# A ConvNeXt-V2 block on one core: rstd by GpSimd's pow, sums of bn_stats on GpSimd, and the yn transfers issued ahead of the input transposes

## The chip, the cores and the metric

The kernel runs on one core of one Trainium2 chip. The metric is the device time in microseconds. Before the change it is 1974.33 us, the median of two runs (1964.08 and 1984.58).

The core has five engines that run their own instruction streams: TensorE (PE in the profile, with PEld for its weight loads), VectorE (DVE), ScalarE (ACT), GpSimd (POOL) and SyncE (SP). Here SP does nothing but issue DMAs and wait on semaphores, in the order of its stream.

## The reference

The input `x` is one image of 512 x 512 pixels with 96 channels, in bf16. What is computed:

```python
out = jnp.zeros_like(x)
for i in range(K):                       # K = 3: a depthwise 3x3 convolution, padded
    for j in range(K):
        out = out + xp[:, i:i+H, j:j+W, :] * dw[i, j][None, None, None, :]
h = _layernorm(out, axis=-1)             # (x - mean) / sqrt(var + 1e-5) over the 96 channels
h = jnp.einsum('bhwc,ce->bhwe', h, w1)   # 96 -> 384
h = _gelu(h)                             # tanh form
gx = jnp.sqrt((h * h).sum(axis=(1, 2), keepdims=True) + 1e-6)   # over all pixels
nx = gx / (gx.mean(axis=-1, keepdims=True) + 1e-6)
h = grn_gamma * (h * nx) + grn_beta + h
h = jnp.einsum('bhwe,ec->bhwc', h, w2)   # 384 -> 96
return x + h
```

The sum in `gx` goes over the whole image, so nothing behind it can start before every pixel has passed the gelu. That splits the kernel into two phases.

## The kernel before

**Blocks and slots.** A block is four image rows (`GR = 4`); there are 128 blocks. Phase 1 is one loop over slots (line 454). Slot s does the convolution of block s and, for earlier blocks, later steps of the pipeline. A table (`at`, lines 422 to 449) gives each step its slot. Every engine's instructions are kept in the order in which the program writes them (the class `InOrder`, lines 25 to 40; the profile puts all of these at line 35). So a step that waits on an engine or on SP holds everything that stands behind it there.

**The steps of phase 1.** In the order of a block's life:

- `load_x` (line 234): SP issues one DMA transpose that brings eight image rows, channels on partitions, into `xT`. One in every second slot, four `xT` buffers; it is issued four slots ahead of the even block with the same rows, and first read by the block before that one.
- `conv_chunks` (line 255): nine taps of 12 matmuls on 32x32 tiles of TensorE add up in one PSUM tile `Y`. `evac` then has ScalarE copy `Y` to `y_bf`, and GpSimd square it into `ysq`. There is one `Y`, so the next convolution waits for its eviction.
- `stage_stats` (line 288): small matmuls sum `y_bf` and `ysq` over channels, into the PSUM tile `S`, for a batch of blocks. Batches have 2, 2, 4 and then 8 blocks (15 of these).
- `stage_chain` (line 302): once per batch VectorE turns the sums into mean and variance, and into rstd by a shift of the float's bits and three Newton steps; then it transposes rstd in 32x32 blocks into `rt`.
- `stage_rows` (line 340): SP writes `rt` to DRAM (four DMAs), one slot after the chain. `stage_bcast` (line 350): SP reads it back onto 32 partitions per image row (four DMAs), two slots later.
- `stage_norm` (line 358): GpSimd multiplies `y_bf` by rstd into `yn`. One slot later `stage_write` (line 366) has SP write `yn` to DRAM, and another slot later `stage_read` (line 369) has SP read it in another layout into one of four `ynT` buffers. The mean's subtraction is folded into the weights `w1p`.
- `mlp_units` (line 376), three slots after the norm: per block six units of two matmuls (96 -> 128 of the 384 features, two image rows), each followed by a gelu on ScalarE into `gt`. After every second unit VectorE takes `bn_stats` of the four rows of `gt`, and, for three blocks in eight (`RECOMP_PATTERN`, line 89: blocks 0, 3 and 6), SP writes `gt` to DRAM. For the others phase 2 computes it again.
- `combine` (line 403): once in eight blocks VectorE turns these statistics into sums of squares.

With batches of eight, block b's MLP is in slot b + 17. Counted modulo 8, the g writes are in slots 1, 4 and 7, the chain in slot 1, the rows in slot 2, the broadcast in slot 4, the combine in slot 0; slot 2 has no channel sums and slot 3 those of two blocks.

**The order within a slot** (lines 457 to 502) is: `load_x` (even slots), writes, reads, broadcasts, norms; then MLP units and convolution taps by turns with the channel sums after the second; then the eviction and `ysq`; then chain, combine and rows. SP therefore sees, in a slot: transpose, yn write, yn read, broadcasts, g writes, rows.

**Phase 2** scales `w2` by the normalisation (lines 512 to 544), loads or recomputes the gelu's output, multiplies by the scaled weights and adds `x`. The change reaches only its first two instructions.

Of the kernel before, what the change touches and what calls it, by code (L numbers as in the profile page):

```python
# [16 lines left out]
NEWTON_ITERS = 3  # L17
LAG_ST = 2
LAG_NORM = 5
LAG_MLP = 3  # L20
# [36 lines left out]
def kernel(  # L57
# [21 lines left out]
    NCH = E // 128  # L79
    NG = W // 128  # L80
    assert H % XR == 0
    NBLK = H // GR
# [80 lines left out]
    NACC = (NBLK + 7) // 8  # L163
    acc = consts.tile([128, NCH, NACC], f32, name="acc")
    nc.vector.memset(acc[:], 0.0)

    grp = {}
    ld_engs = [nc.sync, nc.gpsimd]
# [39 lines left out]
    with ExitStack() as p1:  # L208
# [25 lines left out]
        def load_x(k):  # L234
            lo = k * XR
            xT = xtpool.tile([128, XR, W], bf16, name="xT")
            npix = XR * W
            is_last = lo + XR == H
            npix_t = npix - 16 if is_last else npix
            dst = xT[:].rearrange("p r w -> p (r w)")  # L240
            src = bass.AP(x_t, x_off + lo * W * C, [[C, npix_t], [1, 128]])
            sp.dma_start_transpose(dst[:, 0:npix_t], src)
            if is_last:
                with nc.allow_non_contiguous_dma("last 16 pixels"):
                    sp.dma_start(out=xT[0:C, XR - 1, W - 16:W],
                                      in_=x[0, H - 1, W - 16:W, :].rearrange("w c -> c w"))
            xT_tiles[k] = xT

        ybf, ysq, yns, ynts, rbcs, Ss, rts = {}, {}, {}, {}, {}, {}, {}
        batch_of = {}  # L250
        for k, (b0, n) in enumerate(BATCHES):
            for b in range(b0, b0 + n):
# [47 lines left out]
                                         start=(i == 0), stop=(i == NI - 1))  # L300

        def stage_chain(k):
            b0, n = BATCHES[k]
            N = n * GR * NG
            NT = (N + 31) // 32 * 32
            S = Ss[k]
            mean = small.tile([128, 128], f32, name="mean")
            dve.tensor_scalar(out=mean[:, :N], in0=S[:, 0, :N], scalar1=1.0 / C, scalar2=None, op0=ALU.mult)
            nmsq = small.tile([128, 128], f32, name="nmsq")
            dve.scalar_tensor_tensor(out=nmsq[:, :N], in0=mean[:, :N], scalar=-1.0, in1=mean[:, :N],  # L310
                                           op0=ALU.mult, op1=ALU.mult)
            var = small.tile([128, 128], f32, name="var")
            dve.scalar_tensor_tensor(out=var[:, :N], in0=S[:, 1, :N], scalar=1.0 / C, in1=nmsq[:, :N],
                                           op0=ALU.mult, op1=ALU.add)
            dve.tensor_scalar(out=var[:, :N], in0=var[:, :N], scalar1=0.0, scalar2=LN_EPS,
                                    op0=ALU.max, op1=ALU.add)
            ri = small.tile([128, 128], i32, name="ri")
            dve.tensor_scalar(out=ri[:, :N], in0=var[:, :N].bitcast(i32), scalar1=1, scalar2=None,
                                    op0=ALU.arith_shift_right)
            dve.tensor_scalar(out=ri[:, :N], in0=ri[:, :N], scalar1=-1, scalar2=0x5F3759DF,  # L320
                                    op0=ALU.mult, op1=ALU.add)
            rcur = ri[:, :N].bitcast(f32)
            rn = None
            for it in range(NEWTON_ITERS):
                t_ = small.tile([128, 128], f32, name="nt")
                dve.scalar_tensor_tensor(out=t_[:, :N], in0=rcur, scalar=-0.5, in1=rcur,
                                               op0=ALU.mult, op1=ALU.mult)
                dve.tensor_tensor(out=t_[:, :N], in0=t_[:, :N], in1=var[:, :N], op=ALU.mult)
                rn = small.tile([128, 128], bf16 if it == NEWTON_ITERS - 1 else f32,
                                name="rstd" if it == NEWTON_ITERS - 1 else "rn")  # L330
                dve.scalar_tensor_tensor(out=rn[:, :N], in0=t_[:, :N], scalar=1.5, in1=rcur,
                                               op0=ALU.add, op1=ALU.mult)
                rcur = rn[:, :N]

            rt = rtpool.tile([128, 128], bf16, name="rt")
            dve.transpose(out=rt[:, :NT], in_=rn[:, :NT])
            rts[k] = rt
            Ss.pop(k)

        def stage_rows(k):  # L340
            b0, n = BATCHES[k]
# [61 lines left out]
        def combine(k):  # L403

            bst = bsts.pop(k)
            nr = min(8, NBLK - 8 * k) * GR
            for j in range(NCH):
                v = bst[:, j, :nr, :].rearrange("p a (h s) -> p a h s", h=2)
                sq = small.tile([128, 32, 2], f32, name="sq")
                dve.scalar_tensor_tensor(out=sq[:, :nr, :], in0=v[:, :, :, 1], scalar=256.0, in1=v[:, :, :, 1],  # L410
                                               op0=ALU.mult, op1=ALU.mult)
                sq2 = small.tile([128, 32, 2], f32, name="sq2")
                dve.scalar_tensor_tensor(out=sq2[:, :nr, :], in0=sq[:, :nr, :], scalar=1.0, in1=v[:, :, :, 2],
                                               op0=ALU.mult, op1=ALU.add, accum_out=acc[:, j, k:k + 1])

        def fill(n):
            U = psU.tile([128, 2, W], f32, name="U")
# [6 lines left out]
        def put(s, what):  # L424
            at.setdefault(s, []).append(what)
# [3 lines left out]
        for k, (b0, n) in enumerate(BATCHES):  # L429
            for b in range(b0, b0 + n):  # L430
                s = b + LAG_ST
                if b == b0:
                    s = max(s, last_stat_slot + 2)
                put(max(s, b + LAG_ST), ("stats", b))
                last_s = max(s, b + LAG_ST)
            last_stat_slot = last_s
            put(last_s, ("chain", k))
            put(last_s + 1, ("rows", k))
            put(last_s + 3, ("bcast", k))
            for b in range(b0, b0 + n):  # L440
                s = max(last_norm + 1, last_s + LAG_NORM)
                last_norm = s
                put(s, ("norm", b))
                put(s + 1, ("write", b))
                put(s + 2, ("read", b))
                put(s + LAG_MLP, ("mlp", b))
                last_slot = s + LAG_MLP
                if b % 8 == 7 or b == NBLK - 1:
                    put(s + LAG_MLP, ("combine", b // 8))

        load_x(0)
        load_x(1)
        fill(FILL_FIRST)
        for s in range(last_slot + 1):
            todo = at.get(s, [])
            get = lambda kind: [v for kk, v in todo if kk == kind]
            if s % 2 == 0 and s // 2 + 2 < H // XR:
                load_x(s // 2 + 2)
            for b in get("write"):
                stage_write(b)  # L460
            for b in get("read"):
                stage_read(b)
            for k in get("bcast"):
                stage_bcast(k)
            for b in get("norm"):
                stage_norm(b)
            units = []
            for b in get("mlp"):
                units += mlp_units(b)
            taps, evac = conv_chunks(s) if s < NBLK else ([], None)  # L470
            for b in get("stats"):
                pass
            stats = [lambda b=b: stage_stats(b) for b in get("stats")]

            order = []
            u, t = list(units), list(taps)
            if not u:
                order += t
                if t:
                    order.append(lambda: fill(FILL_EARLY))  # L480
                order += stats
            else:
                k = 0
                while u or t:
                    if u:
                        order.append(u.pop(0))
                    n = 2 - k % 2
                    order += t[:n]
                    t = t[n:]
                    if k == 1:  # L490
                        order += stats
                    k += 1
            for f in order:
                f()
            if evac:
                evac()
            for k in get("chain"):
                stage_chain(k)
            for k in get("combine"):
                combine(k)  # L500
            for k in get("rows"):
                stage_rows(k)

        for q in range(NPRE0):
# [7 lines left out]
    with ExitStack() as pg:  # L512
        gsm = pg.enter_context(tc.tile_pool(name="gsm", bufs=1))
        psG = pg.enter_context(tc.tile_pool(name="psG", bufs=1, space=bass.MemoryType.PSUM))
        ssq = gsm.tile([128, NCH], f32, name="ssq")
        nc.vector.tensor_reduce(out=ssq[:], in_=acc[:], axis=AX.X, op=ALU.add)
        gx = gsm.tile([128, NCH], f32, name="gx")
        nc.scalar.activation(out=gx[:], in_=ssq[:], func=ACTF.Sqrt, bias=eps_t[:], scale=1.0)
        rs_ = gsm.tile([128, 1], f32, name="rs_")
# [101 lines left out]
```

## Time and profile before

One execution was taken by the profiler, with a time of 1976.21 us by the same measure as the runs.

| | us |
|---|---|
| median of the runs | 1974.33 |
| profiled execution | 1976.21 |
| its span, first to last instruction | 1974.2 |
| phase 1, about | 0 to 1400 |
| VectorE busy / in phase 1 | 1672.3 / 1202.1 |
| ScalarE busy / in phase 1 | 1401.3 / 942.2 |
| TensorE (PE) busy / in phase 1 | 1536.8 / 1017.1 |
| GpSimd busy / in phase 1 | 858.3 / 752.5 |
| granted TensorE clock, mean | 0.862 of full speed |

How to read the lines: in a list of groups a row names the engine, the operation, its output and inputs (out<-in, with their shapes), how often it ran, its busy time, its mean duration in ns, and the idle time of the engine before it with what ended that. In a timeline the first two numbers are start and duration in us from the span's start; SPq is a DMA issue on SP, and its duration is that of issuing, not of the transfer. In a table of stretches each row gives, for one stretch, its length and the busy time of each engine with the number of instructions, in the order PE, PEld, DVE, ACT, POOL, then the granted clock, the share of the DMA engines, and GB/s. In a list of waits a row gives us in total and how many times. A busy PE isn't a PE at full speed: a matmul lasts longer at the lower clock.

### The profile page before, as it was taken

The numbers are of one execution on the slowest core, as the hardware profiler recorded it, in microseconds if no ns is written. First come the engines' busy times: TensorE is split into PE (matmuls) and PEld (weight loads), VectorE is DVE, ScalarE is ACT, GpSimd is POOL, SyncE is SP. The second block draws the span as 40 slices with busy tenths as digits, with TensorE's granted clock in tenths as the row PEclk, the third lists the DMA queues.
The fourth block names the chain that finished last, engine by engine and source line by source line (L and its number), as shares of the span: only waits on it lengthen the run. The fifth ranks groups of instructions, "written<-read, shape, count | busy, mean of one in ns | idle before, by whom it ended". The sixth has DMA issues, their size and how long they took to land. (4 is left out here: it accounts for less than half of the span.)

```text
span 1974.2 us, 58644 instructions
## 1 busy us (share of the span) xinstructions
PE 1536.8 (78%) x25396; PEld 687.7 (35%) x25642; DVE 1672.3 (85%) x2646; ACT 1401.3 (71%) x1381; POOL 858.3 (43%) x467
## 2 busy tenths in 40 slices
PE   7577767777777878777777777755599999999998
PEld 4223222222222222222222221211366666666666
DVE  4645998889899898989999999899888888888887
ACT  2455686676777666677686786877578888788887
POOL 5545565645555545565555655551211111112110
PEclk9778797887788777778797897988799999999999
DMA  7878777677675866857778586475699999999995
GB/s 145 167 182 179 204 204 188 177 225 202 179 207 170 221 177 196 221 172 199 195 225 210 172 242 184 155 237 169 236 384 367 366 374 362 376 366 369 371 367 228
DMA packets 466867, 472.17 MB, mean 239 GB/s; under 512 B 292432, under 2 KB 388784, under 8 KB 466608
## 3 DMA queue, kind: packets, MB, share of 16 engines
q1 hardware_dynamic: 414000, 348.86, 60.5%
q0 software_dynamic: 20608, 88.09, 12.0%
q10 hardware_dynamic: 32000, 31.46, 5.1%
q8 instruction: 200, 3.28, 0.7%
q14 instruction: 59, 0.48, 0.1%
HBM read 224.55 MB, written 176.69 MB: 203 GB/s over the span
## 5 line engine op out<-in xcount | busy, mean ns | idle before, releaser
L35 DVE BATCH_NORM_STATS2 bst<-gt 128x6 f32<-128x512 bf16 x1536 | 926.1, 678 | 151.6 <-ACT gt L35 147.7
L35 ACT ACTIVATE gt<-U 128x1024 bf16<-128x1024 f32 x768 | 773.4, 1027 | 372.1 <-PE U L35 166.2
L35 PE MATMUL U<-ynT,w1p 128*128 128x512 bf16 x1307 | 505.8, 462 | 185.4 <-DMA ynT<-yn_dram 145.5
L35 PE MATMUL Y<-xT,Wd 32*32 32x512 bf16 x13806 | 466.4, 450 | 172.7 <-ACT y_bf L35 116.5
L35 POOL TENSOR_TENSOR ysq<-y_bf 128x1536 bf16<-128x1536 bf16 x128 | 351.7, 2748 | 534.5 <-ACT y_bf L35 505.1
L200 ACT ACTIVATE gl<-U 128x1024 bf16<-128x1024 f32 x480 | 457.5, 1028 | 106.0 <-PE U L198 97.5
L35 POOL TENSOR_TENSOR yn<-y_bf,rbc 128x1536 bf16<-128x1536 bf16 x128 | 396.3, 3099 | 29.7 <-DMA yn_dram<-yn 16.8
L570 PE MATMUL O<-W2s,gl 128*128 128x96 bf16 x6096 | 350.4, 206 | 19.8 <-ACT gl L200 5.1
L570 PEld LDWEIGHTS <-gl 128*128 128x128 bf16 x6096 | 304.1, 97 | 140.4 <-ACT gl L200 54.1
L572 DVE TENSOR_TENSOR o_sb<-O,xb 128x384 bf16<-128x384 f32 x512 | 257.1, 552 | 95.8 <-PE O L570 95.6
L35 PEld LDWEIGHTS <-Wd 32*32 32x32 bf16 x13806 | 130.7, 90 | 513.4 <-issue 507.2
L198 PE MATMUL U<-ynl,w1p 96*128 96x512 bf16 x960 | 283.4, 379 | 29.9 <-ACT gl L200 27.8
L184 POOL DMA_DIRECT2D xr<-in_x_dram x127 | 68.6, 540 | 487.5 <-DVE xb L561 371.4
L35 PEld LDWEIGHTS <-w1p 128*128 128x128 bf16 x1536 | 100.3, 101 | 481.2 <-issue 308.1
L35 ACT ACTIVATE y_bf<-Y 128x1536 bf16<-128x1536 f32 x128 | 185.2, 1447 | 64.2 <-PE Y L35 61.3
L561 DVE TENSOR_TENSOR xb<-xr,B2bc_f 128x1536 f32<-128x1536 bf16 x127 | 222.8, 1755 | 3.7 <-DMA xr<-in_x_dram 1.0
L198 PEld LDWEIGHTS <-w1p 96*128 96x128 bf16 x960 | 76.6, 98 | 66.7 <-issue 48.6
L35 PEld LDWEIGHTS <-y_bf 128*128 128x128 bf16 x1536 | 50.1, 100 | 37.2 <-issue 34.5
L35 PE MATMUL S<-rowsel,y_bf 128*128 128x4 bf16 x1536 | 59.5, 168 | 0.0
L35 PE MATMUL S<-rowsel,ysq 128*128 128x4 bf16 x1536 | 57.8, 167 | 0.0
L35 DVE SCALAR_TENSOR_TENSOR sq<-sq,bst 128x64 f32<-128x64 f32 x48 | 47.9, 999 | 1.6
L35 PEld LDWEIGHTS <-ysq 128*128 128x128 bf16 x1536 | 49.3, 100 | 0.0
(64 smaller groups left out, 346.7 us busy)
## 6 DMA issues: line engine op xcount, KB each, us to landing
g_dram<-gt SPq DMA_DIRECT2D x144, 512.0 KB, 3.3
yn_dram<-yn SPq DMA_DIRECT2D x128, 384.0 KB, 4.1
ynT<-yn_dram SPq DMA_DIRECT2D x128, 384.0 KB, 4.5
out_dram<-o_sb SPq DMA_DIRECT2D x128, 384.0 KB, 6.9
xr<-in_x_dram POOLq DMA_DIRECT2D x127, 384.0 KB, 6.9
gl<-g_dram POOLq DMA_DIRECT2D x71, 512.0 KB, 9.1
gl<-g_dram SPq DMA_DIRECT2D x70, 512.0 KB, 9.1
ynl<-yn_dram ACTq DMA_DIRECT2D x80, 384.0 KB, 9.9
```

The costliest lines, as they stand in the source:

```text
L35: r = f(*a, **k)
L184: nc.gpsimd.dma_start(out=xr[:], in_=x[0, r0:r0 + GR].rearrange("r w c -> (r w) c").rearrange("(p g) c -> p g c", g=PXP))
L198: nc.tensor.matmul(U[:, i, :], lhsT=w1p[:C, j * 128:(j + 1) * 128], rhs=ynt[:, i0 + i, :], start=True, stop=True)
L200: nc.scalar.activation(out=perm_view(gts[j][:, :], i0, 2), in_=perm_src(U[:]), func=ACTF.Gelu_apprx_tanh)
L561: nc.vector.tensor_tensor(out=xb[:], in0=xr[:], in1=B2bc_f[:, None, :].to_broadcast([128, PXP, C]), op=ALU.add)
L570: nc.tensor.matmul(O[:, gl_, :], lhsT=gts[j][:, gg * 128:(gg + 1) * 128], rhs=W2s[:, j, :], start=(j == 0), stop=(j == NCH - 1))
L572: nc.vector.tensor_tensor(out=o_sb[:, sub * GPS:(sub + 1) * GPS, :], in0=O[:], in1=xb[:, sub * GPS:(sub + 1) * GPS, :], op=ALU.add)
```

## The change

Four things are edited.

1. The chain on VectorE ends with the variance. Its operations read `S` in PSUM where they read `mean` twice. A new step `stage_pow` on GpSimd, in the same slot, adds epsilon and raises to the power -0.5. A new step `stage_turn`, in the slot of the rows and just ahead of them, has VectorE transpose rstd.
2. The combine moves from VectorE to GpSimd, and one slot later. It adds all squares of means and all variance terms of 8 blocks into two accumulators of 192 elements instead of reducing each; the reduction is done once, at the start of phase 2.
3. In each slot `load_x` is issued behind the yn writes and reads and the broadcasts, no longer ahead of them.
4. The loop runs one slot longer, for the last combine.

```diff
+    accm = consts.tile([128, NCH, 32, 2], f32, name="accm")
+    nc.gpsimd.memset(accm[:], 0.0)
+    accv = consts.tile([128, NCH, 32, 2], f32, name="accv")
+    nc.gpsimd.memset(accv[:], 0.0)
+    mhalf = consts.tile([128, 128], f32, name="mhalf")
+    nc.gpsimd.memset(mhalf[:], -0.5)
...
         def stage_chain(k):
...
-            dve.scalar_tensor_tensor(out=nmsq[:, :N], in0=mean[:, :N], scalar=-1.0, in1=mean[:, :N],
-                                           op0=ALU.mult, op1=ALU.mult)
+            dve.scalar_tensor_tensor(out=nmsq[:, :N], in0=S[:, 0, :N], scalar=-1.0 / C, in1=mean[:, :N],
+                                     op0=ALU.mult, op1=ALU.mult)
             var = small.tile([128, 128], f32, name="var")
             dve.scalar_tensor_tensor(out=var[:, :N], in0=S[:, 1, :N], scalar=1.0 / C, in1=nmsq[:, :N],
...
-            dve.tensor_scalar(out=var[:, :N], in0=var[:, :N], scalar1=0.0, scalar2=LN_EPS,
-                                    op0=ALU.max, op1=ALU.add)
-            ri = small.tile([128, 128], i32, name="ri")
...
-            for it in range(NEWTON_ITERS):
...
+            vars_[k] = var
+
+        def stage_pow(k):
...
+            vare = small.tile([128, 128], f32, name="vare")
+            pool.tensor_scalar(out=vare[:, :N], in0=var[:, :N], scalar1=0.0, scalar2=LN_EPS,
+                               op0=ALU.max, op1=ALU.add)
+            rstd = small.tile([128, 128], bf16, name="rstd")
+            pool.tensor_tensor(out=rstd[:, :N], in0=vare[:, :N], in1=mhalf[:, :N], op=ALU.pow)
+            rstds[k] = rstd
+
+        def stage_turn(k):
...
             rt = rtpool.tile([128, 128], bf16, name="rt")
-            dve.transpose(out=rt[:, :NT], in_=rn[:, :NT])
+            dve.transpose(out=rt[:, :N], in_=rstds.pop(k)[:, :N])
             rts[k] = rt
...
         def combine(k):
...
-            for j in range(NCH):
...
-                dve.scalar_tensor_tensor(out=sq[:, :nr, :], in0=v[:, :, :, 1], scalar=256.0, in1=v[:, :, :, 1],
-                                               op0=ALU.mult, op1=ALU.mult)
...
-                dve.scalar_tensor_tensor(out=sq2[:, :nr, :], in0=sq[:, :nr, :], scalar=1.0, in1=v[:, :, :, 2],
-                                               op0=ALU.mult, op1=ALU.add, accum_out=acc[:, j, k:k + 1])
+            v = bst[:, :, :nr, :].rearrange("p j a (h s) -> p j a h s", h=2)
+            sq = small.tile([128, NCH, 32, 2], f32, name="sq")
+            pool.tensor_tensor(out=sq[:, :, :nr, :], in0=v[:, :, :, :, 1], in1=v[:, :, :, :, 1], op=ALU.mult)
+            pool.tensor_tensor(out=accm[:, :, :nr, :], in0=accm[:, :, :nr, :], in1=sq[:, :, :nr, :], op=ALU.add)
+            pool.tensor_tensor(out=accv[:, :, :nr, :], in0=accv[:, :, :nr, :], in1=v[:, :, :, :, 2], op=ALU.add)
...
-                    put(s + LAG_MLP, ("combine", b // 8))
+                    put(s + LAG_MLP + 1, ("combine", b // 8))
...
-        for s in range(last_slot + 1):
+        for s in range(last_slot + 2):
...
-            if s % 2 == 0 and s // 2 + 2 < H // XR:
-                load_x(s // 2 + 2)
             for b in get("write"):
                 stage_write(b)
             for b in get("read"):
                 stage_read(b)
             for k in get("bcast"):
                 stage_bcast(k)
+            if s % 2 == 0 and s // 2 + 2 < H // XR:
+                load_x(s // 2 + 2)
...
             for k in get("chain"):
                 stage_chain(k)
+            for k in get("chain"):
+                stage_pow(k)
             for k in get("combine"):
                 combine(k)
             for k in get("rows"):
+                stage_turn(k)
                 stage_rows(k)
...
-        nc.vector.tensor_reduce(out=ssq[:], in_=acc[:], axis=AX.X, op=ALU.add)
+        nc.vector.scalar_tensor_tensor(out=accv[:], in0=accm[:], scalar=256.0, in1=accv[:], op0=ALU.mult, op1=ALU.add)
+        nc.vector.tensor_reduce(out=ssq[:], in_=accv[:].rearrange("p j a h -> p j (a h)"), axis=AX.X, op=ALU.add)
```

More of the change, by code (lines that the diff above doesn't have):

```diff
@@ L16 @@
 GRN_EPS = 1e-6
-NEWTON_ITERS = 3
 LAG_ST = 2
@@ L161 @@
                                        op0=ALU.mult, op1=ALU.add)
-    NACC = (NBLK + 7) // 8
-    acc = consts.tile([128, NCH, NACC], f32, name="acc")
-    nc.vector.memset(acc[:], 0.0)
+    accm = consts.tile([128, NCH, 32, 2], f32, name="accm")
[4 more added lines that the diff above has]
+    nc.gpsimd.memset(mhalf[:], -0.5)
     grp = {}
@@ L247, in load_x @@
             xT_tiles[k] = xT
-        ybf, ysq, yns, ynts, rbcs, Ss, rts = {}, {}, {}, {}, {}, {}, {}
+        ybf, ysq, yns, ynts, rbcs, Ss, rts, vars_, rstds = ({} for _ in range(9))
         batch_of = {}
@@ L304, in stage_chain @@
             N = n * GR * NG
-            NT = (N + 31) // 32 * 32
-            S = Ss[k]
+            S = Ss.pop(k)
             mean = small.tile([128, 128], f32, name="mean")
@@ L309, in stage_chain @@
             nmsq = small.tile([128, 128], f32, name="nmsq")
-            dve.scalar_tensor_tensor(out=nmsq[:, :N], in0=mean[:, :N], scalar=-1.0, in1=mean[:, :N],
-                                           op0=ALU.mult, op1=ALU.mult)
+            dve.scalar_tensor_tensor(out=nmsq[:, :N], in0=S[:, 0, :N], scalar=-1.0 / C, in1=mean[:, :N],
+                                     op0=ALU.mult, op1=ALU.mult)
             var = small.tile([128, 128], f32, name="var")
             dve.scalar_tensor_tensor(out=var[:, :N], in0=S[:, 1, :N], scalar=1.0 / C, in1=nmsq[:, :N],
-                                           op0=ALU.mult, op1=ALU.add)
@@ L315, in stage_chain @@
-            dve.tensor_scalar(out=var[:, :N], in0=var[:, :N], scalar1=0.0, scalar2=LN_EPS,
-                                    op0=ALU.max, op1=ALU.add)
-            ri = small.tile([128, 128], i32, name="ri")
[L318 to L321, printed above, removed]
@@ L322, in stage_chain @@
-            rcur = ri[:, :N].bitcast(f32)
-            rn = None
-            for it in range(NEWTON_ITERS):
-                t_ = small.tile([128, 128], f32, name="nt")
-                dve.scalar_tensor_tensor(out=t_[:, :N], in0=rcur, scalar=-0.5, in1=rcur,
-                                               op0=ALU.mult, op1=ALU.mult)
[L328 to L333, printed above, removed]
+                                     op0=ALU.mult, op1=ALU.add)
@@ new lines, in stage_chain @@
+            vars_[k] = var
+        def stage_pow(k):
+            b0, n = BATCHES[k]
+            N = n * GR * NG
+            var = vars_.pop(k)
+            vare = small.tile([128, 128], f32, name="vare")
[4 more added lines that the diff above has]
+            rstds[k] = rstd
@@ L335, in stage_chain @@
+        def stage_turn(k):
+            b0, n = BATCHES[k]
+            N = n * GR * NG
             rt = rtpool.tile([128, 128], bf16, name="rt")
-            dve.transpose(out=rt[:, :NT], in_=rn[:, :NT])
+            dve.transpose(out=rt[:, :N], in_=rstds.pop(k)[:, :N])
             rts[k] = rt
-            Ss.pop(k)
         def stage_rows(k):
@@ L406, in combine @@
             nr = min(8, NBLK - 8 * k) * GR
-            for j in range(NCH):
-                v = bst[:, j, :nr, :].rearrange("p a (h s) -> p a h s", h=2)
-                sq = small.tile([128, 32, 2], f32, name="sq")
-                dve.scalar_tensor_tensor(out=sq[:, :nr, :], in0=v[:, :, :, 1], scalar=256.0, in1=v[:, :, :, 1],
-                                               op0=ALU.mult, op1=ALU.mult)
-                sq2 = small.tile([128, 32, 2], f32, name="sq2")
-                dve.scalar_tensor_tensor(out=sq2[:, :nr, :], in0=sq[:, :nr, :], scalar=1.0, in1=v[:, :, :, 2],
-                                               op0=ALU.mult, op1=ALU.add, accum_out=acc[:, j, k:k + 1])
+            v = bst[:, :, :nr, :].rearrange("p j a (h s) -> p j a h s", h=2)
[3 more added lines that the diff above has]
+            pool.tensor_tensor(out=accv[:, :, :nr, :], in0=accv[:, :, :nr, :], in1=v[:, :, :, :, 2], op=ALU.add)
         def fill(n):
```

## The prediction

> **What bounds the kernel now.** The page comes first. Phase 1 (slices 1 to 28, some 1400 us) and phase 2 have different limits; the change touches phase 1 alone, and only through what its queues carry.
>
> ```profile
> span 1974.2 us, 58644 instructions
> PE 1536.8 (78%) x25396; PEld 687.7 (35%) x25642; DVE 1672.3 (85%) x2646; ACT 1401.3 (71%) x1381; POOL 858.3 (43%) x467
> ...
> PEclk9778797887788777778797897988799999999999
> ```
>
> VectorE looks like the bound, but a share of the span doesn't say which wait ends last. So I went to the slots. In the timeline a slot runs from one eviction of Y (y_bf) to the next. Between the 17th and the last eviction, 136.3 to 1257.05 us, lie 111 slots, 10.10 us each. The table by stretches puts a free slot beside two held ones (slots 94, 105, 107):
>
> ```profile
> core 0: us, PE busy (x) PEld busy (x) DVE busy (x) ACT busy (x) POOL busy (x), PEclk, DMA share, GB/s
> 929.13:937.36 8.23, 6.37 (x142) 2.24 (x144) 7.32 (x14) 7.29 (x8) 5.79 (x2) 1.00 0.58 211
> 1024.40:1036.41 12.01, 9.37 (x144) 2.48 (x147) 11.91 (x22) 7.48 (x8) 5.80 (x2) 0.72 0.49 177
> 1044.04:1057.26 13.22, 9.23 (x166) 2.91 (x168) 12.84 (x20) 7.48 (x9) 5.84 (x2) 0.74 0.23 64
> ```
>
> A free slot takes 8.22 us; in it all 12 bn_stats fit VectorE (7.1 us). A held slot takes 12 to 13 us at a lower TensorE clock. What holds it is the tile view of ynT in that stretch:
>
> ```profile
>   DMA ynT<-yn_dram: 106.1, 38
> ```
>
> TensorE waits for the read of yn in 38 of 111 slots, 2.8 us each. Sorted by slot number modulo 8, these are slots 1, 3 and 4. The timeline of SP shows why:
>
> ```profile
> 870.24 6.75 SPq L35 DMA_DIRECT2D g_dram<-gt  x3
> 877.08 5.00 SPq L35 DMA_TRANSPOSE xT<-in_x_dram  x1
> 882.13 0.57 SPq L35 DMA_DIRECT2D yn_dram<-yn  x1
> 882.79 0.39 SPq L35 DMA_DIRECT2D ynT<-yn_dram  x1
> 893.67 1.75 SPq L35 DMA_DIRECT2D r_dram<-rt  x4
> 895.52 0.38 SPq L35 DMA_DIRECT2D yn_dram<-yn  x1
> 896.00 0.36 SPq L35 DMA_DIRECT2D ynT<-yn_dram  x1
> ```
>
> SP issues in order. The g writes (MLP blocks 0, 3, 6 of 8, so slots 1, 4, 7) hold it until ScalarE's last gelu, the end of the slot. Where an even slot follows (2 and 0), the transpose's 4.6 to 5 us of issuing stand ahead of write and read: the read goes out about 6 us into the slot, lands 4.5 us later, and the next slot waits. The third stall, slot 4, is the rows: SP stood from 883.2 to 893.7 for rt. VectorE shows where rt was:
>
> ```profile
> 880.98 0.27 DVE L35 TENSOR_SCALAR mean<-S 128x128 f32<-128x128 f32 x1
> 881.29 2.71 DVE L35 SCALAR_TENSOR_TENSOR nmsq<-mean 128x128 f32<-128x128 f32 x1
> 884.03 0.29 DVE L35 SCALAR_TENSOR_TENSOR var<-S,nmsq 128x128 f32<-128x128 f32 x1
> ...
> 885.79 2.78 DVE L35 SCALAR_TENSOR_TENSOR rn<-nt,ri 128x128 f32<-128x128 f32 x1
> 888.61 3.06 DVE L35 SCALAR_TENSOR_TENSOR nt<-rn 128x128 f32<-128x128 f32 x1
> ...
> 893.34 0.31 DVE L35 STREAM_TRANSPOSE rt<-rstd 128x128 bf16<-128x128 bf16 x1
> ```
>
> The chain takes 12.7 us where its 16 operations at their short times would take 4.5. The long ones (2.7 to 3.1 us) end when GpSimd's ysq or yn ends.
>
> **What the Trainium skill says.** "SBUF — State Buffer", section "SBUF: two separate sides": VectorE operations with two SBUF inputs or in a 2-port mode and GpSimd take one port pair by turns, each for a whole instruction. The trace agrees: nmsq 2.71, var<-S,nmsq with one input in PSUM always 0.29. "TensorE: Matmul & The Clock Gate", Part 1: an idle window of about 3.4 us halves the clock. The stretches agree (1.00 against 0.72), and the 73 slots without a read stall average 8.97, not 8.22: 32 of them show the low clock without any DMA wait, after the 1.56 us that each slot waits for its Y eviction. "GPSIMD Engine Reference", sections 3.1 and 7: a two-input fp32 operation of 2048 elements takes 4497 ns, and inner steps over 8 bytes cost half more; used below. No page prices pow.
>
> **The change part by part.**
>
> *VectorE.* Of each of 18 chains 12 operations go, 4 stay (mean, nmsq, var, transpose); the six combine operations and three accumulator reads per eight blocks go. By the groups of equal shapes: 86 us of combine (47.9 + 34.2 + 3.9), 130 of removed 128-wide chain operations, 16 by nmsq (1.34 to 0.29), 27 of the narrower batches: 259 us, so DVE busy about 1414. This isn't the gain: most of it lay beside slots that waited for SP. It counts in two places. In the tail (after the last Y eviction at 1257.05, with bn_stats ending at 1397.58, 140.5 us) VectorE is busy 139.65, so it bounds: 17 blocks of 12 x 0.593 (the distance of bn_stats starts) are 121, plus 3 for filling: **-16 us**. The other place is rt, next.
>
> *rt and rows.* The turn is now behind slot 2's bn_stats. These end 2.9 us after the slot's last gelu in free slots, so rt is at 3.3 us of slot 3; rows 1.75 us; write at 5.2, read at 5.7, landed at 10.2. Slot 4 asks for it at about 8.3 (slot 3 has two blocks' stats, 9.0 long). A stall of 1.9 us stays, where it was 3.3.
>
> *Write and read ahead of the transpose.* In slots 0 and 2 the read goes out about 0.7 us into the slot and lands at 5.2, 3 us before need: both stalls go. The transposes leave 1 us later (in slot 4 with four bcasts ahead 3.6 us later); their tile is first read three slots on, so 8 us and more cover that. The write waits for yn, which ends 7.4 us into the slot before, so it rarely holds SP.
>
> Sum of the steady part: 14 slots remain held, at the held average 12.27 less the 0.9 by which the stall is below the 2.8 mean, 11.4; 97 at 8.97. 97 x 8.97 + 14 x 11.4 = 1030 against 1121: **-91 us**. I keep the 44% of clock dips of unheld slots, as nothing in the change removes their cause.
>
> *Startup* (to 136.3). The narrow chains take 8, 7 and 16 us; the last ends in rt at 73.97, and SP waits from 66 for it. In slot 12 the transpose (83.84 to 90.64) stands ahead of read 2, which landed at 103.2 behind it. Without both, MLP block 2 starts some 19 us earlier, the next ones lose part of that again to the bcasts and transpose that come behind; I take **-15 us**, bounds 0 and -25. The 16 us in which POOL waits for the preload of g stay.
>
> *GpSimd.* It has 2.4 us of each free slot idle. In slot 1 of 8 come vare, pow and three combine operations of 192 elements. From the page's 2.2 ns each and half more for the 12-byte step: an estimate of 0.4 to 0.65 us, 2 us for three; vare 0.3. **pow** is in no trace: from below 0.3 us (128 elements as a multiplication), from above nothing but the rival below; I take 2.5, near the geometric middle of 0.3 and 20. Together 4.8 us behind ysq and ahead of slot 2's yn. Queued behind are that yn (done at 3.9 us of slot 3 instead of 7.4 of slot 2), and then its write, which stands behind rows (5.2) anyway: hidden up to 6 us, so a pow of 3.5 is free, then each us is a us of stall, 16 times. A cost below nothing is excluded: it's work added.
>
> *End.* The last combine is now POOL after bn_stats (2 us and two handovers) and one more VectorE operation, against six VectorE operations in 2.9: **+2 us**. The three memsets on GpSimd stand beside the first loads, 10 us before it has work: nothing.
>
> The profiled execution took 1976.2 (span 1974.2), 1.9 above the median of two runs 20 us apart. 1976.2 - 91 - 16 - 15 + 2 = 1856; I say **1855**.
>
> **The rivals.**
> *pow is slow* (slower). Past 3.5 us each us delays yn, its write and the read behind it, 16 times. The gain of 121 is gone at 3.5 + 121/16 = 11.1 us, or 87 ns an element; 2% slower from 13.6. At 20 us: 1855 + 16 x 16.5 = 2119. For it: an operation of GpSimd that nothing prices. Against it: ysq and yn pass two inputs at 1.8 to 2.0 ns an element, so 87 would be over forty multiplications. 0.08.
> *The reads land late all the same.* DMA is busy 0.71 to 0.78 over eight slots and over 1.0 in some; bcasts and transposes landed 7 to 9 us after issue at 902 to 913. If the two freed reads lose 2 us each in such queues, 28 x 2 = 56 come back: 1911. For it: 15 MB must pass in less time. Against: in slots 0 and 2 the share before the read is low. 0.15.
> *The clock dips go too.* With fewer stalls the clock stays up: eight slots at 65.8 + 2.7 = 68.5, 950 for the part, 171 less: 1776. For it: runs of free slots from 991 to 1024. Against: dips that follow no stall. 0.17.
> *It doesn't do what it says*: SP, held by g writes and rows, stays the pace, and only tail and startup gain part: 1955. 0.07.
>
> **How the numbers follow.** The forecast has 0.53, own range 1815 to 1890. Leaving out the slow pow and the change that does nothing (0.15) and the far ends, the range runs from the dips' case to the late reads' case with its spread: 1765 to 1915. Faster than 2%, about what a measurement can tell from no change, is the forecast, the dips and most of the late reads: 0.83; the same 0.08; slower 0.09.
>
> **What would show it.** Right: stalls on ynT down from 106 to about 30 us in the same stretch, in slot 4 alone; eight slots in 73 to 75 us; VectorE near 1414, nmsq at 0.29; in the SP timeline the transpose behind the read; the tail near 124. Wrong: POOL standing for more than 3.5 us on pow; reads that land 7 us after issue in even slots; ynT stalls in slots 1 and 3; or a mean of unheld slots far from 8.97.

## The result and the profile after

The changed kernel takes 2183.64 us, the median of two runs (2178.57 and 2188.70), against 1974.33 us before: a ratio of 1.106 with a 95% interval of 1.079 to 1.133. It is slower. Some executions of a kernel run in a slower state at a lower granted clock; every ratio here, and the time given for the reordering alone, comes from fast ones. The page of the profiled execution, engines and granted clock:

```profile
span 2186.9 us, 58307 instructions
PE 1554.0 (71%) x25396; PEld 689.6 (32%) x25642; DVE 1430.5 (65%) x2286; ACT 1400.6 (64%) x1381; POOL 1228.3 (56%) x554
...
PEclk9877776867879577687867677786979999999999
```

VectorE lost 242 us of work and GpSimd gained 370. The groups of GpSimd's instructions in the changed kernel tell where these are:

```profile
L34 POOL TENSOR_TENSOR rstd<-vare,mhalf 128x128 bf16<-128x128 f32 x15 | 312.0, 20798 | 1.3
...
L34 POOL TENSOR_TENSOR rstd<-vare,mhalf 128x32 bf16<-128x32 f32 x2 | 10.9, 5464 | 0.2
L34 POOL TENSOR_TENSOR rstd<-vare,mhalf 128x64 bf16<-128x64 f32 x1 | 10.6, 10570 | 0.1
L34 POOL TENSOR_TENSOR accv<-accv,bst 128x192 f32<-128x192 f32 x16 | 10.2, 638 | 0.0
L34 POOL TENSOR_SCALAR vare<-var 128x128 f32<-128x128 f32 x15 | 9.7, 646 | 7.7 <-DVE bst L34 7.7
L34 POOL TENSOR_TENSOR sq<-bst 128x192 f32<-128x192 f32 x16 | 9.7, 606 | 59.0 <-DVE bst L34 59.0
L34 POOL TENSOR_TENSOR accm<-accm,sq 128x192 f32<-128x192 f32 x16 | 9.4, 588 | 1.3
```

One pow of 128 columns takes 20.80 us; 32, 64 and 128 columns give a straight line, 0.36 us and 0.16 us a column. A multiplication of the same shape, in an experiment below, takes 0.46 us. The three combine operations cost what was estimated (1.8 us for 2); vare took 0.65 us where 0.3 was taken.

What a pow does shows in the timeline of GpSimd, in slots 1 to 4 of one batch:

```profile
512.73 2.75 POOL L34 TENSOR_TENSOR ysq<-y_bf 128x1536 bf16<-128x1536 bf16 x1 [5.11 <-ACT y_bf L34]
515.44 0.64 POOL L34 TENSOR_SCALAR vare<-var 128x128 f32<-128x128 f32 x1
516.17 20.79 POOL L34 TENSOR_TENSOR rstd<-vare,mhalf 128x128 bf16<-128x128 f32 x1
...
538.68 3.08 POOL L34 TENSOR_TENSOR yn<-y_bf,rbc 128x1536 bf16<-128x1536 bf16 x1
541.72 2.74 POOL L34 TENSOR_TENSOR ysq<-y_bf 128x1536 bf16<-128x1536 bf16 x1
```

The timeline of SP over the same stretch:

```profile
512.23 0.73 SPq L34 DMA_DIRECT2D ynT<-yn_dram  x1
513.06 5.61 SPq L34 DMA_TRANSPOSE xT<-in_x_dram  x1
537.33 1.74 SPq L34 DMA_DIRECT2D r_dram<-rt  x4
541.78 0.34 SPq L34 DMA_DIRECT2D yn_dram<-yn  x1
542.23 0.37 SPq L34 DMA_DIRECT2D ynT<-yn_dram  x1
```

And the timeline of VectorE:

```profile
514.04 0.29 DVE L34 SCALAR_TENSOR_TENSOR nmsq<-S,mean 128x128 f32<-128x128 f32 x1
514.36 0.29 DVE L34 SCALAR_TENSOR_TENSOR var<-S,nmsq 128x128 f32<-128x128 f32 x1
...
536.99 0.31 DVE L34 STREAM_TRANSPOSE rt<-rstd 128x128 bf16<-128x128 bf16 x1 [14.81 <-POOL rstd L34]
```

The transpose stands behind write and read now, as meant (513.06), and VectorE's short chain is as meant too: nmsq takes 0.29 us where it took 2.71. That agrees with the Trainium skill, "SBUF — State Buffer", "SBUF: two separate sides": with one input in PSUM it doesn't take turns with GpSimd. But SP stands from 518.7 to 537.3 for rt, issues the rows, and then stands from 539.1 to 541.8 for yn, which stood behind pow. So pow makes two things late, one of them by way of VectorE. The table by stretches has a slot 2, this slot 4, and a slot 6:

```profile
511.20:518.82 7.62, 5.76 (x118) 1.64 (x120) 7.10 (x14) 7.21 (x8) 6.01 (x3) 1.00 0.98 260
527.65:556.63 28.98, 9.86 (x144) 2.52 (x147) 12.09 (x21) 7.49 (x9) 25.53 (x9) 0.59 0.41 95
564.85:580.12 15.27, 10.16 (x144) 2.51 (x147) 7.93 (x14) 7.48 (x8) 5.79 (x2) 0.66 0.99 244
```

Slot 4 takes 29 us instead of 12.5. The tile view of ynT, between the same two evictions as before (now at 132.0 and 1452.9 us):

```profile
  DMA ynT<-yn_dram: 274.2, 28
```

So the waits are fewer, 28 instead of 38, and 9.8 us each instead of 2.8. By slot number modulo 8, the means in us from the timelines (13 or 14 slots each; the columns on the right are experiments told of below):

| slot | before | after | multiplication | Newton in PSUM | repeated | broadcasts later |
|---|---|---|---|---|---|---|
| 1 | 11.0 | 10.5 | 10.1 | 10.4 | 9.2 | 9.1 |
| 3 | 12.5 | 11.3 | 10.9 | 11.0 | 8.8 | 9.1 |
| 4 | 12.5 | 25.8 | 10.3 | 10.1 | 8.3 | 8.3 |
| 6 | 8.3 | 12.8 | 9.6 | 9.9 | 13.3 | 8.4 |
| others, mean | 9.1 | 8.7 | 8.8 | 8.7 | 7.9 | 7.9 |

### The profile page after: what moved, and what is told of

It reads as the page before. It is cut to its first block, busy times and chain, and to the rows that moved or that the text cites. A ratio compares the mean times of both kernels' runs of the same rounds, so it can differ in the third digit from the quotient of the medians.

```text
span 2186.9 us, 58307 instructions
## 1 busy us (share of the span) xinstructions
PE 1554.0 (71%) x25396; PEld 689.6 (32%) x25642; DVE 1430.5 (65%) x2286; ACT 1400.6 (64%) x1381; POOL 1228.3 (56%) x554
## 5 line engine op out<-in xcount | busy, mean ns | idle before, releaser
L34 PE MATMUL U<-ynT,w1p 128*128 128x512 bf16 x1307 | 518.3, 472 | 363.9 <-DMA ynT<-yn_dram 336.6
L34 PE MATMUL Y<-xT,Wd 32*32 32x512 bf16 x13806 | 474.7, 458 | 184.6 <-ACT y_bf L34 129.7
L34 POOL TENSOR_TENSOR rstd<-vare,mhalf 128x128 bf16<-128x128 f32 (+2 forms) x18 | 333.5, 18526 | 1.5
L34 DVE STREAM_TRANSPOSE rt<-rstd 128x128 bf16<-128x128 bf16 (+2 forms) x18 | 5.3, 297 | 256.6 <-POOL rstd L34 256.6
## 6 DMA issues: line engine op xcount, KB each, us to landing
gl<-g_dram SPq DMA_DIRECT2D x70, 512.0 KB, 10.3
```

The source lines that it names most:

```text
L34: r = f(*a, **k)
```

## The experiments

**The multiplication.** My theory: the loss is the length of pow alone. The rival: the new order on SP and the sums on GpSimd cost too. This kernel leaves out rstd: it has a product in its place.

```diff
-            pool.tensor_tensor(out=rstd[:, :N], in0=vare[:, :N], in1=mhalf[:, :N], op=ALU.pow)
+            pool.tensor_tensor(out=rstd[:, :N], in0=vare[:, :N], in1=mhalf[:, :N], op=ALU.mult)
```

> The changed kernel with a multiplication by -0.5 in the place of the power, so rstd is left out; everything else is as in the change. Theory (the whole loss is the 20.8 us that one pow takes): the multiplication takes about 0.5 us, and the prediction's own sum for a free pow holds: 1855 us, between 1820 and 1890; waits on ynT in the steady part near 30 us instead of 275; VectorE's wait for rstd under 10 us. Rival (the new order on SP and the sums on GpSimd cost too): above 1930 us, with reads that land late in slots 1, 3 or 6 of 8.

Measured: 1899.9 us, ratio to before 0.963 (0.957 to 0.969); the profiled span is 1890.4. Pow therefore costs 284 us of medians and turns a gain of 3.7% into the loss. Of the 296.5 us between the profiled spans, 13.9 lie in the startup, 261.8 between the evictions and 21.1 in the tail; the end is 0.3 shorter. The tile view of ynT in this kernel, between the same two evictions, has the waits down to

```profile
  DMA ynT<-yn_dram: 35.8, 19
```

as expected in size, but not in place, so the size is luck in part: the prediction had some 30 us in slot 4 alone, and here slot 4 has 9.7, slot 6 17.1 and slots 1 and 3 9.0. The late reads in slot 6 are a sign that the rival named. VectorE's wait for rstd is 9.3 us, under the 10 stated. The time lies 10 us above the stated 1820 to 1890, below the rival's 1930: most of the theory holds, and the missing 45 us against 1855 are taken up further below.

**Pow kept, its result not used.** A slow pow can hold TensorE in two ways: yn and ysq queue behind it on GpSimd, or rt, rows and SP wait for its result. This kernel too leaves out rstd: it takes the product, and runs pow behind it into a tile that nobody reads.

```diff
-            pool.tensor_tensor(out=rstd[:, :N], in0=vare[:, :N], in1=mhalf[:, :N], op=ALU.pow)
+            pool.tensor_tensor(out=rstd[:, :N], in0=vare[:, :N], in1=mhalf[:, :N], op=ALU.mult)
+            spare = small.tile([128, 128], bf16, name="spare")
+            pool.tensor_tensor(out=spare[:, :N], in0=vare[:, :N], in1=mhalf[:, :N], op=ALU.pow)
```

> As the kernel with the multiplication, but the pow runs behind it on GpSimd into a tile that nobody reads; rstd is left out. It parts the two ways in which a slow pow can hold TensorE. Theory A (the queue: yn and ysq stand behind the pow on GpSimd): 2140 to 2190 us, VectorE's wait for rstd gone, waits on ynT still over 240 us. Theory B (the data: rt waits for rstd, the rows for rt, SP for the rows): below 1950 us, waits on ynT under 80 us.

Measured: 2199.19 us, 1.113 (1.108 to 1.119). The wait of VectorE for rstd, 256.6 us over 18 waits in the changed kernel, is all but gone here, in the tile view of rt:

```profile
  POOL rstd L34: 16.5, 3
```

and the tile view of ynT has the waits as they were:

```profile
  DMA ynT<-yn_dram: 273.0, 32
```

So the queue is enough: rt comes 3.4 us into slot 3 instead of 17.7 (means of 14 slots), and nothing is gained, as yn is late all the same. The wait of VectorE for POOL rstd lies beside that and adds nothing to it. (The time is 9 us above the range stated for it.)

The reverse isn't shown: no run has rt late and yn free. The trace of the changed kernel says what to expect of it. There the rows end 19.5 us into slot 3 (6.3 with the multiplication), the write of yn goes out at 21.5 and the read at 22.3 (medians). With yn in time the late rows would still hold the write until 19.5, so an estimate from these times is that only 2 to 3 of some 15 us would be saved. By this estimate either way alone makes nearly the whole loss; for the queue it is shown.

**The reordering alone**, in the kernel before:

```diff
-            if s % 2 == 0 and s // 2 + 2 < H // XR:
-                load_x(s // 2 + 2)
             for b in get("write"):
...
                 stage_bcast(k)
+            if s % 2 == 0 and s // 2 + 2 < H // XR:
+                load_x(s // 2 + 2)
```

> The kernel before with nothing changed but the place of the transposes, behind write, read and broadcasts. Theory (the transpose's issue ahead of the read made the stalls of slots 1 and 3): 28 stalls of 2.9 us go, 81 us, and about 10 in the startup: 1885 us, waits on ynT from 106 to 30 to 50 us, left in slot 4. Rival (VectorE's chain and SP's wait for rt set the pace): over 1945 us, with the stall of slot 4 grown by what the others lost.

Measured: 1947.1 us, 0.986 (0.978 to 0.993), from two runs; whether that is a gain of 2% is unclear. The time is 62 us above the theory's and just on the rival's side. Slot 1 is shorter (9.8 us for 11.0) and slot 3 too (11.1 for 12.5), but slot 4 takes 14.8 where it took 12.5, and in the tile view of ynT the waits fall only to

```profile
  DMA ynT<-yn_dram: 84.9, 24
```

The chain is what it was. SP doesn't wait longer for rt; in SP's list of waits between the evictions, of the kernel before and of this one, it stands a little less:

```profile
SPq L35 <- DVE rt L35: 135.9, 14, 11.1
SPq L35 <- DVE rt L35: 120.5, 14, 10.2
```

But rt still comes 7.9 us into slot 3 (7.8 before), and the read behind the rows lands 14.6 us into it (14.3). Slot 3 ends 1.4 us sooner, so slot 4 only stands longer for the same read: 64.5 us over the 14 slots instead of 40.9. Of the 38 us between the two profiled spans the startup alone gives 17: the 17th eviction is at 119.0 instead of 136.3 us.

**The short chain without the reordering**: the multiplication's kernel with `load_x` back at the head of the slot (the last diff reversed), and rstd left out.

> The kernel with the multiplication, and the transposes again ahead of write and read; rstd is left out. It is the change without its reordering and without the price of pow. Theory (the reordering frees slots 1 and 3, and only together with an early rt is it worth its full amount): against the kernel with the multiplication the startup's 18 us and the stalls of slots 1 and 3 come back, 28 times some 2.5 us less what the later queue gives back: 1950 us, 1930 to 1975. Rival (the shorter work on VectorE made the gain): 1890 to 1915 us, as with the reordering.

Measured: 1949.92 us, 0.993 (0.991 to 0.996), inside the range of the theory and far from the rival. Slots 1 and 3 are long again (11.7 and 12.0 us), with 59.0 of the 72.7 us of waits on ynT. Alone, the two halves of the change bring 1.4% and 0.7%; together, without pow, 3.7%. The slots agree: each edit frees a wait on SP, and what the one frees goes in part into the wait that the other one leaves.

**Newton steps in PSUM.** Can rstd be had without pow and without the stretches? The chain goes back to VectorE, with variance and iterate in the two quarters of the bank that `S` leaves free, so that no operation has two SBUF inputs:

```diff
-                Ss[k] = psS.tile([128, 2, 128], f32, name="S")
+                Ss[k] = psS.tile([128, 4, 128], f32, name="S")
...
+            dve.tensor_scalar(out=V[:, :N], in0=S[:, 2, :N], scalar1=0.0, scalar2=LN_EPS, op0=ALU.max, op1=ALU.add)
+            dve.tensor_scalar(out=R.bitcast(i32), in0=V[:, :N].bitcast(i32), scalar1=1, scalar2=None,
+                              op0=ALU.arith_shift_right)
+            dve.tensor_scalar(out=R.bitcast(i32), in0=R.bitcast(i32), scalar1=-1, scalar2=0x5F3759DF,
+                              op0=ALU.mult, op1=ALU.add)
+            for it in range(3):
...
+                dve.scalar_tensor_tensor(out=t_[:, :N], in0=R, scalar=-0.5, in1=V[:, :N], op0=ALU.mult, op1=ALU.mult)
...
+                dve.tensor_tensor(out=t2[:, :N], in0=t_[:, :N], in1=R, op=ALU.mult)
+                if it < 2:
+                    dve.scalar_tensor_tensor(out=R, in0=t2[:, :N], scalar=1.5, in1=R, op0=ALU.add, op1=ALU.mult)
...
```

(`V` is in SBUF and `R = S[:, 3, :N]` in PSUM; the last step writes rstd in SBUF, and its transpose follows at once.)

> The changed kernel, with rstd by the Newton steps on VectorE again, but written so that no operation has two inputs in SBUF (variance and iterate lie in two free quarters of the bank of S), and with the transpose of rstd at the end of this chain. It computes the whole reference. Theory: a chain of 16 operations at 0.2 to 0.3 us, 5 us without stretches; rt is ready before the rows' place in SP's order, so the stall in slot 4 goes too: 1820 us, 1790 to 1850, waits on ynT under 20 us. Rival (5 us more of VectorE per batch push bn_stats and the gelu's buffers): not faster than the kernel with the multiplication.

Measured: 1888.23 us, 0.955 (0.951 to 0.959). The chain, from VectorE's timeline, first and last lines:

```profile
584.93 0.27 DVE L34 TENSOR_SCALAR mean<-S 128x128 f32<-128x128 f32 x1
585.24 0.29 DVE L34 SCALAR_TENSOR_TENSOR nmsq<-S,mean 128x128 f32<-128x128 f32 x1
...
589.49 0.29 DVE L34 SCALAR_TENSOR_TENSOR rstd<-nt,S 128x128 bf16<-128x128 f32 x1
589.81 0.31 DVE L34 STREAM_TRANSPOSE rt<-rstd 128x128 bf16<-128x128 bf16 x1
```

All 16 operations take 5.2 us, where the chain of before took 12.7 and pow alone 20.8. Waits on ynT fall to 22.0 us. But 1820 was missed by 68: stalls were exchanged for something else. The 103 slots that wait for no transfer have a mean of 9.29 us, while 73 such slots before had 8.97; 54 of the 103 show the low clock. And slot 6 has waits of its own in 4 of 14. Two experiments take these one by one.

**Repeated matmuls.** In each slot TensorE waits 1.56 us for the eviction of Y, right after the first MLP unit. If that gap brings the clock down, work in it should keep it up:

```diff
-                for i in range(2):
+                for i in (0, 1, 0, 1, 0, 1) if (i0 == 0 and j == 0) else (0, 1):
                     pe.matmul(U[:, i, :], lhsT=w1p[:, j * 128:(j + 1) * 128],
                                      rhs=ynts[b][:, i0 + i, :], start=True, stop=True)
```

> The kernel with the Newton steps in PSUM, and in each slot the first two matmuls of the MLP are run three times over into the same place (the last counts), while TensorE would wait for the eviction of Y. It computes the whole reference. Theory (the slots of 10.9 us without a wait on a transfer come from the clock, which falls after a stretch with the 1.56 us wait in it): the four extra matmuls fill 0.9 us of that wait, the low clock becomes rare, the mean of slots without a transfer wait falls from 9.3 to under 8.6 us, and the time to 1810 to 1840 us. Rival (those slots are long for another reason, or the power allows no more): 1880 us or longer by the added work.

Measured: 1816.75 us, 0.928 (0.922 to 0.933), as the theory said. Added work made the kernel faster, by 71 us of medians. From the table by stretches, between the 17th and the last eviction, of the Newton kernel:

```profile
119.33:1175.02 1055.69, 874.43 (x15983) 259.34 (x15982) 840.57 (x1504) 789.88 (x753) 656.00 (x259) 0.83 0.85 209
```

and of the kernel with repeated matmuls:

```profile
114.41:1102.56 988.15, 849.68 (x16413) 295.94 (x16412) 833.00 (x1504) 787.20 (x753) 657.81 (x259) 0.96 0.89 224
```

The granted clock goes from 0.83 to 0.96, and TensorE with more matmuls is busy for less time. Of the wait for the eviction 0.70 us is left (median). None of the 86 slots without a transfer wait has the low clock any more; their mean is 8.09 us.

The same edit **in the kernel before**:

> The kernel before, with nothing changed but the first two matmuls of each block's MLP run three times over. It computes the whole reference. Theory (the low clock of slots that wait for no transfer is a loss of its own, beside the stalls): the 73 such slots fall from 8.97 to about 8.2 us, 55 us in all, while the 38 held slots keep their waits: 1920 us, 1900 to 1940. Rival (SP and VectorE set the pace there, so slots that get shorter only lengthen the waits on ynT): over 1950 us, with the waits on ynT grown from 106 by about as much as the other slots lost.

Measured: 1954.28 us, 0.992 (0.989 to 0.995). The slots without a wait are 7.86 us, so the first half of the theory holds; yet the tile view of ynT shows

```profile
  DMA ynT<-yn_dram: 166.3, 55
```

instead of 106.1 in 38 waits. The rival was right on the time: SP's late reads set the pace there, and what TensorE gained it spends waiting for them.

**Broadcasts later.** In the kernel with repeated matmuls slot 6 takes 13.3 us, and has 63.3 of the 74.8 us of waits on ynT. The reason is already in the SP timeline of the Newton kernel, from slot 4 on:

```profile
599.14 1.90 SPq L34 DMA_DIRECT2D rbc<-r_dram  x4
601.08 9.72 SPq L34 DMA_TRANSPOSE xT<-in_x_dram  x1
610.91 1.96 SPq L34 DMA_DIRECT2D g_dram<-gt  x3
612.96 1.15 SPq L34 DMA_DIRECT2D yn_dram<-yn  x1
614.20 1.14 SPq L34 DMA_DIRECT2D ynT<-yn_dram  x1
```

Behind the broadcasts the transpose takes 9.7 us to issue, so slot 4's g writes and slot 5's write and read go out late: the read at 614.2, 5.7 us into slot 5. With repeated matmuls slot 4's transpose takes 9.3 us on the mean, the others 5.4 to 6.6. The edit moves the broadcasts to slot 5, which has no transpose:

```diff
-            put(last_s + 3, ("bcast", k))
+            put(last_s + 4, ("bcast", k))
```

> The kernel with the repeated matmuls, and the four broadcasts of rstd one slot later, in slot 5, which has no transpose. It computes the whole reference. Theory (in slot 4 broadcasts and transpose stand together on SP, the transpose takes 8 to 10 us to issue, and the read for slot 6 leaves late): the waits of 4 to 5 us in slot 6 go; 14 slots, about half of them held: 20 to 40 us less than without the move. Rival (the broadcasts now land late for yn): the waits on ynT grow.

Measured: 1752.72 us, 0.895 (0.889 to 0.900), 64 us less than without the move, more than the 20 to 40 expected: as slots had become shorter, slot 6 was held in 12 of 14 batches. It now takes 8.4 us, slot 4's transpose 5.4 to issue, and slot 6's, which is now the first behind the broadcasts, 8.2. In the tile view of ynT the waits are

```profile
  DMA ynT<-yn_dram: 15.5, 15
```

This kernel computes the whole reference and is faster than both: 221.6 us below the 1974.33 of before, 431 below the changed one.

**Pow in slices.** Last, whether pow's amount of work or its lump did the harm. Each block's 16 columns go through mean, variance and pow in the slot of its channel sums:

```diff
+            for b in get("stats"):
+                stage_part(b)
             for k in get("chain"):
-                stage_chain(k)
-            for k in get("chain"):
-                stage_pow(k)
+                Ss.pop(k)
```

(`stage_part` has the operations of `stage_chain` and `stage_pow`, on the 16 columns of block b.)

> The changed kernel with the same number of elements through pow, but cut: each block's 16 columns get mean, variance and pow in the slot of the block's channel sums, 16 columns in 0.36 + 16 x 0.16 = 2.9 us, eight times where there was one of 20.8. It computes the whole reference. Theory (the lump in front of yn made the loss, not the amount of GpSimd's work): GpSimd is busy some 9.2 us per slot, which is about the mean slot of the kernel with the multiplication: 1900 to 1950 us. Rival (the amount of pow's work costs as such): over 2050 us.

Measured: 1958.52 us, 0.997 (0.994 to 1.000): 8 us above the range, well below the rival. The same elements pass through pow, in 128 pieces of 2.92 us. Of the 284 us that pow cost, 225 came from its being one piece and 59 remain. These aren't the amount of pow's work alone: the smaller operations' starts are in them, and a wait that the kernel with the multiplication doesn't have. In the list of waits between the evictions TensorE's channel sums stand for VectorE, which still reads the same tile `S`:

```profile
PE S L34 <- DVE var L34: 21.7, 48, 0.9
```

The table by stretches, for this kernel between the same evictions, shows GpSimd as the fifth engine:

```profile
131.60:1231.61 1100.01, 894.45 (x15983) 263.72 (x15982) 834.25 (x1627) 791.59 (x753) 1011.75 (x484) 0.81 0.80 201
```

It is busy 1012 of 1100 us, 92%, so it has little slack left. Cut up, pow only equals the kernel before; how much of that is GpSimd's load and how much the new wait, no run parts.

## Why the prediction was wrong

**Pow** is the term that was mis-sized: 2.5 us taken, 20.8 measured, eight times as much. The bounds were open above, and the middle of 0.3 and 20 was no estimate but a guess; the argument against a long one (that it would be over forty multiplications) was none, since nothing says that a pow is few of them; against the 0.46 us of a multiplication of the same shape it is forty-five. The mechanism was the one that the first rival names: yn queued behind pow, its write and the read behind it, in slot 4. What the rival leaves out is that rt and the rows come late by the same pow, almost as much. By its own rule, a microsecond for each past 3.5, 16 times, 20.8 gives 277 us; 284 were measured. That they are so close is luck in part: the rule puts 17.3 us into each slot 4, where it was 15.5, and the rest came where the rule has nothing, 3.2 us in each slot 6. The rival's sum ended at 2119 only because it stood on 1855 and on 20.0 us. A chance of 0.08 for it was far too low for an operation without a price on which the sign depended.

**Write and read ahead of the transpose**: the mechanism holds, but not by itself, as the reordering alone showed. The prediction counted both freed stalls in full because it took rt to be early at once; that holds for the change without pow.

**rt and rows**: right in kind. In the multiplication's kernel rt comes 3.5 us into slot 3 (3.3 in the sum), and the read lands at 11.0 (10.2). Slot 4 is still only 10.3 us, below the 11.4 of the sum, because slot 3 lasted 10.9 us and not 9.0, so slot 4 asked later.

**"Their tile is first read three slots on, so 8 us and more cover that"** is a step that failed. It asked who reads the transposed tile, not what is queued behind the transpose on SP: in slot 4, with four broadcasts ahead, that is slot 5's write and read. Slot 6 went from 8.3 to 9.6 us without pow and to 12.8 with it; in the kernel with repeated matmuls it was 13.3, and moving the broadcasts took that to 8.4.

**The unheld slots at 8.97**: nothing in the change removes the dips, that was right; of the slots that wait for no transfer 44 of 93 show the low clock without pow, 32 of 73 before. But such a slot took 10.7 us instead of 10.2, and 93 slots at 9.20 came out: 0.23 more on each is 21 us of the 29 by which the part between the evictions was missed; the rest is four more held slots than the 14 of the sum. Why the low ones got longer is open. The repeated matmuls show that these dips follow the wait for Y and not transfers.

**The smaller parts**, from the kernel with the multiplication: startup -18 (predicted -15), tail -10.5 (-16), the part between -62 (-91), the end +6.5 (+2); the sum is -84 instead of -120, and so 1890 in the profiled execution. The missing 5.5 us of the tail stay open. At the end the cost is for the most part not the sums on GpSimd (the first scaled weights come 11.4 us after the last bn_stats, 5.4 before): two of phase 2's xb operations, 1.75 us each and one of them behind a 2.9 us wait for xr, now come between the reduction and the weights. VectorE's busy time (1430.5 for 1414) and nmsq (0.29) came out as said. (The landings that the rival of the late reads gives as 7 to 9 us are 6.1 to 9.9 in the trace; nothing rests on that.)

**The rival of the clock dips** (1776 with 0.17): the dips went only with an edit of their own, and the time came below 1776 only with a second one, the broadcasts'.

## What to carry to other kernels

An operation that no page and no trace prices, put into an in-order queue that a short loop leans on, needs its price first: one run on the chip would have shown 0.16 us a column. Where it is known to be long, cut it to pieces that fit the queue's slack in one slot: here that took back 225 of 284 us. Ask both what stands behind it in its queue and who waits for its result; here the two were late by nearly the same, and an early result alone gained nothing. And of a transfer that is moved in a queue, ask what is now behind it, besides when its own data are needed: two edits that each free one of several waits in series can show next to nothing alone.

## What the runs showed of the hardware

- GpSimd's pow with fp32 inputs takes 0.36 us and 0.16 us for each column of 128 partitions: 2.92 us for 16, 5.46 for 32, 10.57 for 64, 20.80 for 128. A multiplication of 128 columns with the same inputs takes 0.46 us; ysq, a multiplication in bf16, 1.8 ns a column.
- With a wait of 1.56 us in each slot, TensorE's clock was low in 32 of 73 slots without a transfer wait in the kernel before, and in 54 of 103 in the Newton kernel; with 0.70 us of that wait left, in none of 86. In the kernel before, between the 17th and the last eviction, the 63 stretches of 3.4 us (the step of the clock's records) after which the clock fell had TensorE busy for a median of 50%; the 138 after which it stayed up, 77%. "TensorE: Matmul & The Clock Gate", Part 1, of the Trainium skill speaks of an idle window; here windows half busy were enough. Four matmuls of 512 columns more per slot raised the granted clock from 0.83 to 0.96 and saved 71 us.
- In the Newton kernel VectorE's operations with one input or the output in PSUM take 0.27 to 0.30 us for 128 columns, the integer steps of the rsqrt included; in none of 15 chains was one stretched, though GpSimd was busy beside 200 of the 225, where nmsq with two inputs in SBUF took up to 2.7 us beside GpSimd.
- The DMA transpose that SP issues next behind the four broadcasts takes longer to issue: 9.3 us on the mean in slot 4 of the kernel with repeated matmuls, where the others take 5.4 to 6.6. With the broadcasts one slot later slot 4's takes 5.4 and slot 6's 8.2.
